# Batches 6 and 7 of the first round: their second product by seven products for eight twice, half of the weights parked in DRAM, and new orders for all engines

## The chip, the cores and the metric

One Trainium2 chip, of which the kernel uses one core: TensorE (PE; its weight loads are shown as PEld), VectorE (DVE), ScalarE (ACT), GpSimd (POOL), and SyncE (SP), which issues most DMAs. The metric is the device time of one execution in microseconds; the median of several runs counts.

## What is computed

Cross attention between tokens and states, then a feed-forward block on its result:

```python
scores = scale * x @ state^T;  a = softmax(scores);   xread = a @ state      # 512 tokens read 32 states
scores2 = scale * state @ x^T; a2 = softmax(scores2); sread = a2 @ x         # 32 states read 512 tokens
X = concatenate([xread, sread]) as (B*S, H*D)        # B = 8, S = 512 + 32, H*D = 512
h = X @ w_in                                         # 512 -> 2048
g = h * erf(softplus(h))
out = g @ w_out                                      # 2048 -> 512
```

All is float32, 8 batches, 8 heads of width 64. The output is (4352, 512).

## The kernel before

Work goes by batches of 512 tokens; the states' 256 rows come as one more piece. The 2048 inner columns are done in two rounds: round one (`u` = 0) takes the first 1024 of them for batches 1 to 7, then for the states; round two (`u` = 1) the other 1024, again for all. Batch 0 is done ahead, in one go, by straight products (L623, L630), while the weights arrive.

For batches 1 to 7 the products are fast ones: a product of 2 x 2 blocks is done by seven block products for eight, from sums of blocks which VectorE makes. In a round, a batch passes through

- the attention (`attend`, `read`, `turn_read`; in round one only), with loads of x on SP (`xq`, 64 KB pieces, and `x`),
- `mixed` (L1125), states times w_in, which stands in for the read of the states,
- `first_product` (L1224), seven block products for eight, into the `ring` (its "h" planes),
- `serf`: softplus, erf and a multiplication (L1246, L1261, L1275), and the sums `sums_a` (L1264),
- the second product, with w_out. The blocks of w_out and the differences of them that this needs are the seven weights `("W", u, 1..7)`; three of them live in tiles called `raw` (`T[1]`, `T[2]`, `T[4]`), the rest in `w_out` itself (L428 makes the differences).

The second product exists in two forms. `second_product` (L1308) does seven block products of 4 x 2 matmuls with 256 columns, 56 in all per batch, adds results in `oo` and stores two halves of the rows from SP (L1328). `twice_product` (L1464) does each of the seven by seven for eight again: 49 products of two matmuls with 128 columns, 98 in all. For this it needs sums of the left factor (four per group, L1446, into scratch views: `yt`, and `wide`, which is `xT`), and 28 differences of the inner weights (`sums_b`, L1373), kept in the half of `w_out` and `raw` that this round does not use. Its results are copied out (L1474), added (L1479, L1513), and seven quarter stores go from POOL as DMAs that accumulate in DRAM (L1508). Before the change round one uses the first form for all its batches and round two the second for all. The last batch of round two joins its results on VectorE and stores from SP.

Between the rounds come the states: `sums_states` and `first_states` (L1627), `second_states` (L1676), `put_states`, with `bring_in` (L1769), which loads the second half of w_in from DRAM (`kept_in`) into `xq` and `x`. Every batch's attention weights and their sums are parked in DRAM in round one (`keep_y`) and brought again in round two (`bring_y`).

The order of work is written out: every operation is entered by `op` with an engine, a cost, what it reads and what it writes; a table `ORDER` gives for each engine the sequence in which its operations stand, and `emit` issues them so. The orders of TensorE, VectorE and ScalarE are kept as written; DMAs wait in line on their queue. Waits come from the tiles' overlaps, not from that table. The page's lines are those of this kernel.

Of the kernel before, what the change touches and what calls it, by code (L numbers as in the profile page):

```python
# [17 lines left out]
def kernel(  # L18
# [47 lines left out]

    ring = const.tile([P, 2, 3, GF, GF, P], F32, name="ring")
# [299 lines left out]
    def mixed_pair(b, gs, first_h=False, split=False, then=lambda: None):  # L367

        for g in gs:
            m_t[b, g] = mix.tile([P, 2, gw], F32, name="m")  # L370
# [70 lines left out]
    def begins(b):  # L441
        return 1 - b % 2
# [143 lines left out]
    def groups0():  # L586
# [12 lines left out]
        def mixed_part(g, first, n, hs=range(H)):  # L599
            if (0, g) not in m_t:  # L600
                m_t[0, g] = mix.tile([P, 2, gw], F32, name="m")
# [84 lines left out]
    def next0():  # L686
# [26 lines left out]
        def mixed(j):  # L713
            g = 2 * begins(1) + j
            if not n_ps:
                for k in range(2):
                    m_t[1, 2 * begins(1) + k] = mix.tile([P, 2, gw], F32, name="m")
# [77 lines left out]
    def op(engine, cost, at, go, reads=(), writes=(), table=None, land=0.0):  # L795
# [9 lines left out]
        for r in writes:  # L805
# [6 lines left out]
            8 2 0 11 10 9 12 3 1 13-15 22 18 17 19 6 16 20 23 7 21 24-26 35-36 31 4-5 27 32-34 60  # L812
            37-39 28 40 47 59 41-43 61-62 48 44-45 49 46 63 66 29 64 51 65 68-69 52-53 70 54 67 71
            50 72 30 73 55-56 74 76 57-58 106 78-79 107 80-81 108 75 109 82-83 110 84-85 113 112 111
            90-91 116 86 77 114 87 117 88 115 92 94 118 89 93 119-120 95 98-99 96 123 121 100-101
            153 125 97 154 126 156 102-104 155 122 157 127-129 158 105 130 159-160 131 133 163 134
            132 164 137-138 162 141 161 139 124 165 140 166 135 167 136 145-146 168 170 142-143
            147-148 200 144 172-173 202 201 203 174 149-150 175 169 207 176 204 177 180 205 151-152
            210 206 181 209 171 211 182 208 184 212 183 213-214 185 178 186 179 187-188 215 217
            189-190 192-193 247 194 191 195 248 219 250 220 216 249 196 251 221 197 222 252 254 253  # L820
            198 227 257 199 256 231 258 255 223 228 260 218 259 232-233 262 229 224 261 230 225 293
            234-235 226 239 236 240 295 241-242 237 294 265 238 266 296 267 263 268 297 269 243 273
            244 270 245 298 300 299 274 302-303 271 264 246 275 304 277 335 301 276 336 306 305 272
            281 337 278-280 339 341 282 340 285 283 338 307 286 342 284 287-288 343 308 344 289 363
            309 345 290-291 310 364 292 346 315 347 316 319 317 348 323 369 320 318 370 321-322 365
            311 367 366 327 371 312 372 313 328 314 368 329 373-377 349 378 324 330 393 325 350 326
            395-396 394 400 353 397 331-332 354 398 333-334 355 403 399 351 359 404 401-402 360 406
            352 405 361 357 408 407 356 358 383 362 437 379-382 387 385 388 384 440 386 389 391 441
            439 438 390 442 444 416 392 409 447 443 446 448 418 445 417 420 410 421 419 450 412 411
            422 449 452 413 430 451 414-415 482 431 481 432 423 433 484 424 483 425 434 426 485 427  # L830
            435 486 488 436 429 428 491 460 487 461 453 492 463 489 462 490 464 454-455 494 456-457
            493 465 496 459 458 466-467 495 469 474 525 471 526 468 476 470 527-528 475 477 529 478
# [3 lines left out]
            583 553 545 554 613 562 546-547 584 563 555 564-565 557 556 558 614 559 616 566 560 617  # L836
            615 561 567 618 620 568 619 585 623 622 586 592 587 624 594 589 596 621 625 590 626-627
            593 588 595 628 597 591 598 657 606 599 658 608 607 601 609 600 659 602 610 660 603 612
            661 611 604-605 663 662 636 629 664 638 630-631 667 632-633 668 637 634 665-666 639 669
            635 640 670 641-643 650 645 644 646-647 651-654 649 655 648 671 656 673 672 674 678 675  # L840
            680 676-677 679 682 685 681 687 686 688 684 689 683 692 691 690 694 693 699 696 695 701
            697 700 703 702 698 704-705""",
        ACT: """
            4 6 5 9 7 1 0 10 8 11 13 12 30-31 15 22-23 16 14 35 17 34 3 36 32 37 33 19 21 18 20 26
            24 41 40 27 38-39 49 28 25 29 2 42-43 53 47 55 54 44 50 56 51 46 45 57 62 59 58 64 63 61
            65 52 67 66 60 69 48 68 70 76 75 71 79 77-78 72 80 73 90 74 91 86 92-93 84 94 99 81-82
            101 83 102 96 105 103 100 85 104 106 97 88 112 95 107 113 98 87 108 116 114-115 117 109
            89 127 110 129 118 128 130 111 120 123 119 121 131 136 138 133 137 139-140 132 141 122
            125 144 135 142 149 143 150 134 145 154 151-153 124 146 164 147 126 165 148 160 166 157
            155 167-168 173 158 156 175-177 174 169 171 186 178 161 187 159 162 172 170 188 190  # L850
            179-180 189 181 191 182-184 201 163 203 185 202 204 195 194 197 205 193 210 192 212-213
            206 196 211 208 214-215 218 223 225 198 224 207 199 226 217 232 209 216 219-220 200
            221-222 234 228 233 235-236 241 227 243 242 244 239 245 248 237 249 229 258 247 238 246
            240 230 250 260 251-252 231 259 261 253-254 262 264 271 266 263 256 265 273 267 274 268
            255 272 269 275 270 277 284 278 287 285 276 279 286 257 289 280-281 290 282-283 291-293
            298 300-301 299 297 294-295 302 312-313 311 306 314 305 304 296 303 307-309 335 288 337
            310 338 336 339 344 315 320 346-347 321 323 341 322 352 316 345 343 350 348 324 340
            317-318 359-360 342 357-358 330 319 349 351 353 381 354 325 355 331 383 382 356 333 326
            332 327 384 328 385 390 334 366 392 329 393 367 361 389 362 388 386 369 368 391 364 363
            370 394 406 387 405 398 397 365 371 395 403-404 372 396 376 427 399-400 374 401-402 373  # L860
# [5 lines left out]
            529 525 536 541 501 507 524 506 527 544 503 508 542-543 534 514 535 509 526 533 565 537  # L866
            515-516 538-539 510 517 567 540 512 566 568 511 518 569 550 513 545 551 574 571 546 576
            548 572 570 549 577 547 575 579 552 573 578 553 581 580 582 554-555 583 556 584 560
            585-586 557 561 558 562-563 559 587 564 588 592 590 589 593 595 591 597 594 598 600 599
            596 602 601 603 607 605 608 604 606 610 609 611""",  # L870
        DVE: """
            0-1 38 16 15 14 17 2-3 39-40 24-26 6-7 4 19 18 21 36-37 20 22-23 5 27-30 32 34 31 33 35
            10 74 52 46 11 51 8 53 50 13 9 42 12 61 43 48 60 75 62 47 77 41 54 56 76 44 58 49 55 57
            59 81 73 63-65 67 45 66 82 69 71 68 72 70 101 83 121 123 78 99 84 100 102 122 79 85 93
# [38 lines left out]
    def emit():  # L913
# [21 lines left out]
        order = sorted(begin, key=lambda n: (begin[n], n))  # L935
        for n in order:
            ops[n][3]()

    made_banks = {}

    def bank(name):
# [916 lines left out]
```

## Time and profile before

| What | Value |
|---|---|
| Time, median of 3 runs | 709.88 us (709.11 to 709.97) |
| The profiled execution: time | 709.91 us |
| its span, first to last instruction | 708.1 us |
| Granted TensorE clock | 1.000 |
| Last matmul's end | 703.5 us |
| Second product of round one, first matmul per batch 1 to 7 | 129.5, 175.5, 218.2, 259.9, 302.9, 342.9, 385.7 us |
| L1308, PE rows (two for each matmul of the source) | 784 of 128x256 |
| L1464, PE rows | 1372 of 128x128 |
| SP's queue | 33.9% of 16 DMA engines' time, 64.25 MB |
| POOL's queue | 12.9%, 11.01 MB, all after 485 us |

The first 100 us are batch 0 and the loading of weights; 100 to about 440 us is round one, with the states' pieces towards its end; from about 470 us round two. A matmul's busy time contains its pipeline, and rows overlap: what one costs is the distance from its start to that of the next.

### The profile page before, as it was taken

What the parts mean: (1) busy time and instruction counts of PE and PEld (TensorE: products, weight loads), DVE (VectorE), ACT (ScalarE), POOL (GpSimd) and SP (SyncE); (2) the same over time, 40 slices, a digit from 0 to 9 for tenths busy, and PEclk for the clock granted to TensorE, in tenths of its full rate; (3) what the DMA queues carried; (4) which work ended last, traced back from release to release, by engine and by line L of the source; (5) the groups of instructions that cost most, each with busy time, mean ns of one, the idle gap of its engine ahead of it and who ended that gap; (6) DMA issues with size and microseconds to landing.
All of it is one profiled execution on the core that took longest, in us unless ns stands there. A gap on an engine that the chain in (4) does not pass through costs nothing.

```text
span 708.1 us, 12453 instructions
## 1 busy us (share of the span) xinstructions
PE 699.9 (99%) x4871; PEld 563.7 (80%) x4871; DVE 539.3 (76%) x852; ACT 465.4 (66%) x782; POOL 51.6 (7%) x48
## 2 busy tenths in 40 slices
PE   8999999999999999999999999999999999999997
PEld 7444346687878788787899988888989898989997
DVE  6997887988969688485735426499768776978897
ACT  4999898958587665757263463738485756666742
POOL 0000000000000000000000000001113222212222
PEclk9999999999999999999999999999999999999999
DMA  8869582756835464353320001104246535526555
GB/s 259 254 193 248 198 187 54 148 94 144 224 90 111 95 170 122 95 174 78 113 82 31 31 23 60 52 31 80 33 82 67 106 34 96 74 33 78 86 89 106
DMA packets 156011, 76.58 MB, mean 108 GB/s; under 512 B 123440, under 2 KB 145456, under 8 KB 155440
## 3 DMA queue, kind: packets, MB, share of 16 engines
q1 hardware_dynamic: 143984, 64.25, 33.9%
q0 software_dynamic: 11424, 11.01, 12.9%
q8 instruction: 38, 0.62, 0.4%
q10 hardware_dynamic: 544, 0.52, 0.2%
q14 instruction: 21, 0.17, 0.1%
HBM read 42.60 MB, written 29.49 MB: 102 GB/s over the span
## 4 chain that ended last, share of the span: by engine, by line
PE 93%; DMA 3%; SPq 1%; ACT 1%; DVE 1%; issue 1%; ACTq 0%; DVEq 0%
PE o L1308 24%; PE o L1464 21%; PE h L1224 16%; PE o L630 7%; PE at L1224 6%; PE o L1676 3%; PE h L1627 3%; PE at L623 2%; PE h L623 2%; PE at L1125 2%; PE h L1125 2%; DMA raw<-in_moe_w_out_dram 2%; SPq L360 1%; PE at L1627 1%; PE at L1087 1%; PE h L984 1%
## 5 line engine op out<-in xcount | busy, mean ns | idle before, releaser
L1236 ACT COPY ring<-h 128x512 f32<-128x512 f32 x112 | 64.8, 587 | 100.5 <-PE h L1224 95.4
L1308 PE MATMUL o<-w_out,ring 128*128 128x256 f32 x448 | 110.3, 381 | 0.0
L1264 DVE TENSOR_TENSOR ring<-ring 128x1024 f32<-128x1024 f32 (+1 forms) x60 | 68.2, 1145 | 42.3 <-ACT ring L1261 42.3
L1308 PEld LDWEIGHTS o<-w_out,ring 128*128 128x128 f32 x448 | 83.4, 190 | 17.5 <-issue 5.9
L1224 PE MATMUL h<-aT,m 128*128 128x256 f32 x336 | 85.9, 380 | 0.0
L1308 PE MATMUL o<-raw,ring 128*128 128x256 f32 x336 | 82.8, 381 | 0.0
L1308 PEld LDWEIGHTS o<-raw,ring 128*128 128x128 f32 x336 | 62.7, 190 | 12.9 <-issue 5.0
L1246 ACT ACTIVATE ring<-ring 128x512 f32<-128x512 f32 x112 | 66.9, 630 | 6.0 <-DVE ring L1242 1.8
L1224 PEld LDWEIGHTS h<-aT,m 128*128 128x128 f32 x336 | 61.6, 190 | 8.2 <-ACT ring L1236 0.3
L1275 DVE TENSOR_TENSOR ring<-ring 128x1024 f32<-128x1024 f32 x56 | 67.8, 1217 | 0.3
L1464 PE MATMUL o<-w_out,w_in 128*128 128x128 f32 x448 | 60.6, 276 | 0.0
L1464 PEld LDWEIGHTS o<-w_out,w_in 128*128 128x128 f32 x448 | 56.5, 192 | 4.4 <-issue 1.7
L630 PE MATMUL o<-w_out,ring 128*128 128x512 f32 x128 | 59.3, 599 | 0.0
L1261 ACT ACTIVATE ring<-ring 128x1024 f32<-128x1024 f32 (+1 forms) x60 | 58.6, 1002 | 0.2
L630 PEld LDWEIGHTS o<-w_out,ring 128*128 128x128 f32 x128 | 23.6, 190 | 28.9 <-issue 27.4
L1464 PE MATMUL o<-w_out,ring 128*128 128x128 f32 x336 | 46.0, 276 | 0.0
L1508 POOL DMA_DIRECT2D out_dram<-ot x6 | 7.9, 1309 | 516.6 <-DVE w_out L1373 484.2
L1464 PEld LDWEIGHTS o<-w_out,ring 128*128 128x128 f32 x336 | 42.5, 192 | 3.2 <-ACT ot L1474 0.8
L1464 PE MATMUL o<-raw,ring 128*128 128x128 f32 x252 | 34.9, 276 | 0.0
L1464 PEld LDWEIGHTS o<-raw,ring 128*128 128x128 f32 x252 | 32.3, 192 | 1.5 <-DVE w_in L1446 0.8
L1238 DVE TENSOR_TENSOR ring<-ring,at 128x512 f32<-128x512 f32 x28 | 19.1, 683 | 17.5 <-ACT ring L1236 6.4
L1464 PE MATMUL o<-raw,xT 128*128 128x128 f32 x224 | 29.3, 276 | 0.0
(268 smaller groups left out, 1301.6 us busy)
## 6 DMA issues: line engine op xcount, KB each, us to landing
raw<-in_moe_w_in_dram SPq DMA_DIRECT2D x16, 512.0 KB, 4.9
raw<-in_moe_w_out_dram SPq DMA_DIRECT2D x8, 1024.0 KB, 5.7
xq<-in_x_dram SPq DMA_DIRECT2D x112, 64.0 KB, 2.6
x<-in_x_dram SPq DMA_DIRECT2D x56, 128.0 KB, 3.4
out_dram<-oo SPq DMA_DIRECT2D x14, 512.0 KB, 3.2
kept_a<-aT SPq DMA_DIRECT2D x7, 512.0 KB, 3.3
aT<-kept_a SPq DMA_DIRECT2D x7, 512.0 KB, 3.3
out_dram<-oo POOLq DMA_DIRECT2D x12, 256.0 KB, 4.6
```

The lines of the kernel that those rows point to most:

```text
L623: nc.tensor.matmul(out=h_t[g, i], lhsT=m_t[0, g][:, e, P * i:P * i + P], rhs=aT[0][:, e], start=start, stop=not start)
L630: nc.tensor.matmul(out=acc[r], lhsT=gT[g][:, i, P * r:P * r + P], rhs=w_out[:, GF * g + i, :], start=(made_of[r] == 1), stop=(made_of[r] = ...
L1125: nc.tensor.matmul(out=bank(names[e])[q, :], lhsT=st[r, b, q], rhs=of_group[2 * u + j][r, :, i, :], start=True, stop=True)
L1224: nc.tensor.matmul(out=out_[:, i], lhsT=x_[:, q:q + P], rhs=y_, start=(start and i == 0), stop=(i == 1), skip_group_check=not start)
L1236: op(ACT, 0.5, t, lambda: nc.scalar.copy(out_(), view(bank(name))), [name], w)
L1246: op(ACT, 0.53, t, lambda: nc.scalar.activation(out=part(splane, k), in_=part(hplane, k), func=ACTF.Softplus), area(hplane, ks=[k], os=[o] ...
L1261: op(ACT, 0.085 + 0.875 * share, at + n, lambda s_=s_: nc.scalar.activation(out=s_, in_=s_, func=ACTF.Erf), [], area(splane, ks=[k], os=os ...
L1264: op(DVE, 0.065 + 1.075 * share, at + n + 1, lambda s_=s_, h_=h_: tt(s_, s_, h_, op=ALU.mult), area(hplane, ks=[k], os=os), area(splane, k ...
L1275: op(DVE, 1.14, at + k, lambda k=k, x_=x_, y_=y_, how=how: tt(get("h", k), get(*x_), get(*y_), op=how), area(v[x_[0]], ks=[x_[1]]) + area( ...
L1308: nc.tensor.matmul(out=view(name)[:, h], lhsT=lhs[:, i, :], rhs=weight_of[n]()[:, u, i, :], start=(start and h == 0 and i == 0), stop=(h = ...
L1464: nc.tensor.matmul(out=out_[:, Q2 * k:Q2 * k + Q2], lhsT=lhs[:, k, i], rhs=rhs[:, i], start=first, stop=(k == len(ns) - 1 and i == 1), ski ...
L1627: nc.tensor.matmul(out=bank(bk)[:, P * i:P * i + P], lhsT=x_[:, i, k], rhs=y_[:, k], start=(start and i == 0 and k == 0), stop=(i == GF - ...
```

## The change

Of batches 6 and 7 in round one the second product is done by `twice_product`. This needs a place for the 28 inner differences, which is the half of `w_out` and `raw` that holds round two's weights. So these weights are made earlier, written to DRAM (`keep_w`, four DMAs on SP, placed when batch 2 is at its second product), and brought back after batch 7 (`bring_w`), before the states' second half. Other scratch: `xq`, the `m` tiles and `xT` for the sums of factors; `oo`, `ot`, `x`, `sc` and an `m` tile for results. The four `m` buffers become one tile `mm_t`, so that neighbouring ones can be used as one; `sums_states` and `first_states` of the first half stand some 11 us earlier and use `aT0` and `oo` in the place of an `m` tile and `xT`. In round one the first store to each quarter of a batch's rows is a plain one from SP, the other three accumulate from POOL. The orders of all five engines are new throughout; the operations entered for other batches are the same.

```diff
+    mm_t = mix.tile([P, 4, 2, GF * P], F32, name="m", bufs=1)
...
-    mt = lambda j: kept_tile("m%d" % j, lambda: mix.tile([P, 2, gw], F32, name="m"))
+    mt = lambda j: mm_t[:, j]
...
-    def sums_b(at):
+    def sums_b(u, at):
         def chunk(n):
-            t = w_out[:, 0:NF // 2].rearrange("p i e -> p (i e)").rearrange(
-                "p (n x) -> p n x", n=4)[:, n - 1] if n < 5 else \
-                T[(1, 2, 4)[n - 5]][:, 0].rearrange("p i e -> p (i e)")
+            t = w_out[:, NF // 2 * (1 - u):NF // 2 * (2 - u)].rearrange(
+                "p i e -> p (i e)").rearrange("p (n x) -> p n x", n=4)[:, n - 1] if n < 5 else \
+                T[(1, 2, 4)[n - 5]][:, 1 - u].rearrange("p i e -> p (i e)")
...
+    kept_w = dram.tile([P, (NF // 2) * d_model + 3 * GF * E2], F32, name="kept_w")
+
+    def weights_of(u):
+        first = NF // 2 * d_model
+        parts = [(w_out[:, NF // 2 * u:NF // 2 * (u + 1)].rearrange("p i e -> p (i e)"),
+                  kept_w[:, 0:first])]
+        for k, n in enumerate((1, 2, 4)):
+            q = first + GF * E2 * k
+            parts.append((T[n][:, u].rearrange("p i e -> p (i e)"), kept_w[:, q:q + GF * E2]))
+        return parts
+
+    W_of = lambda u: [("W", u, n) for n in range(1, 8)]
+    B_of = lambda u: [("B", u, n, m) for n in range(1, 8) for m in range(4, 8)]
+
+    def keep_w(at):
+        op(SP, 2.4, at, lambda: [nc.sync.dma_start(out=k, in_=t) for t, k in weights_of(1)],
+           W_of(1), ["kept_w"], land=16.0)
+
+    def bring_w(at):
+        op(SP, 2.4, at, lambda: [nc.sync.dma_start(out=t, in_=k) for t, k in weights_of(1)],
+           ["kept_w"], W_of(1) + B_of(0), land=16.0)
+
-    def twice_product(b, splane, hplane, inner, at, at_s, final=None):
+    def twice_product(b, u, splane, hplane, inner, at, at_s, final=None):
...
+        else:
+            first = lambda: static["xq"].rearrange("p i m d -> p (i m d)").rearrange(
+                "p (x m i t) -> p x m i t", x=2, m=4, i=2) if par == 0 else \
+                mm_t[:, 0:2].rearrange("p x e (m i t) -> p x (e m) i t", m=2, i=2)
+            yt = lambda x0, x1: first() if x0 == 0 else mt(3).rearrange(
+                "p e f -> p (e f)").rearrange("p (x m i t) -> p x m i t", x=1, m=4, i=2)
...
+            elif not u and not par:
+                t = static["x"].rearrange("p (z c) h d -> p z (c h d)", z=2)[:, g - 2].rearrange(
+                    "p (x e) -> p x e", x=2)
...
-        def put(v, r, c, t):
+        def put(v, r, c, t, plain=False):
+            if plain and not u:
+                op(SP, 0.5, t, lambda: nc.sync.dma_start(out=quad(r, c), in_=one(v)),
+                   every(*v), [("out", b, r, c)], land=3.5)
+                return
...
-        put(R1, 0, 0, at + 8)
-        put(R4, 1, 0, at + 11)
+        put(R1, 0, 0, at + 8, True)
+        put(R4, 1, 0, at + 11, True)
...
-        put(R3, 0, 1, t)
+        put(R3, 0, 1, t, True)
         put(R7, 1, 0, t)
-        put(R5, 1, 1, t)
+        put(R5, 1, 1, t, True)
...
-        if u == 0:
+        if u == 0 and b < TWICE:
             second_product(b, u, splane, hplane, base, at_s)
         else:
-            twice_product(b, splane, hplane, inner, base, at_s,
-                          3 - hplane if b == B - 1 else None)
+            twice_product(b, u, splane, hplane, inner[u], base, at_s,
+                          3 - hplane if u and b == B - 1 else None)
+        after(base)
...
+    TWICE = B - 2
...
             if b == 2:
                 sums_w(1, base + 20, 1, 2, 4, 3)
+                keep_w(base + 30)
...
-                first_states(0, 0, nxt - U + 14, names[0])
+                first_states(0, 0, nxt - U + 3, names[0])
+        if b == TWICE:
+            adopt(W_of(1), B_of(0))
+            inner[0] = sums_b(0, base - 10)
...
     second_states(0, 0, base)
+    bring_w(base)
```

`adopt(names, into)` enters no operation any more; it makes later users of one set of names wait for those of the other.

More of the change, by code (lines that the diff above doesn't have):

```diff
@@ L817 @@
[L817 to L827, printed above, removed]
@@ L937, in emit, with adopt @@
             ops[n][3]()
+    def adopt(names, into):
+        every = [*names, *into]
+        used = sorted({n for r in every for n in [*wrote.get(r, ()), *seen.get(r, ())]})
+        for r in every:
+            wrote[r], seen[r] = used, []
     made_banks = {}
@@ L1438, in place @@
                 if m in (5, 6, 7, 3):
-                    return [("Y", slot, m)]
+                    return [("Y", 0, 4, m)] if not u and par and not slot else [("Y", u, slot, m)]
                 h, ih = {1: (0, 0), 2: (0, 1), 8: (1, 0), 9: (1, 1)}[m]
@@ L1469, in mm @@
                 op(PE, 0.447 * len(ns), t, go,
-                   place(9 if m == 4 else m) + [("W", 1, n) if m < 4 else ("B", n, m) for n in ns],
+                   place(9 if m == 4 else m) + [("W", u, n) if m < 4 else ("B", u, n, m) for n in ns],
                    [of_bank[to]])
@@ L1729, with unit @@
     sums_w(0, BASE, 1, 2, 4, 3)
-    def unit(b, u, base, splane, hplane, follow, between):
+    def unit(b, u, base, splane, hplane, follow, between, after=lambda base: None):
         at_s = base + 14
@@ L1743 @@
     hp = {b: 2 if b % 2 else 0 for b in range(1, B)}
+    TWICE = B - 2
+    sums = (3, 5, 6, 7)
+    parts = lambda par, g: [("R", par, g, x_, h, q) for x_ in range(2) for h in range(2)
+                            for q in range(2)]
+    inner, names = {}, {}
     for b in range(1, B):
@@ L1770, in bring_in @@
                                           in_=kept_in[:, GF * j:GF * j + GF])
-                op(SP, 0.2, base + 4, bring_in, [],
-                   ["x", "xq"] + ["xq%d" % i for i in range(NI)] + ["w_in10", "w_in11"], land=8.0)
-                names[0] = sums_states(0, base + 4)
-                sums_reads(base + 8)
-        names = {}
+                    op(SP, 0.5, base + 4, bring_in, [], [k, "w_in1%d" % j] + used, land=7.0)
+                adopt([("Y", 0, 1, m) for m in sums], [("mS", 1, 0), ("mS", 1, 1)])
+                adopt(parts(0, 0), ["oo00", "oo01"])
+                names[0] = sums_states(0, base - 8)
+                sums_reads(base - 6)
         def follow(nxt, b=b):
@@ L1782, in follow @@
             else:
-                first_states(0, 0, nxt - U + 14, names[0])
-        unit(b, 0, base, 1, hp[b], follow, between)
+                first_states(0, 0, nxt - U + 3, names[0])
+        if b == TWICE:
+            adopt(W_of(1), B_of(0))
+            inner[0] = sums_b(0, base - 10)
+            adopt(["xq"] + ["xq%d" % i for i in range(NI)], [("Y", 0, 0, m) for m in sums])
+            adopt(["xT%d" % k for k in range(4)], [("Y", 0, 2, m) for m in sums])
+            for par in range(2):
+                adopt(["oo%d%d" % (r, c) for r in range(2) for c in range(2)], parts(par, 0))
+            adopt([("mS", 0, e) for e in range(2)], parts(1, 2))
+        if b == B - 1:
+            adopt(["m%d%d" % (j, e) for j in range(2) for e in range(2)],
+                  [("Y", 0, 4, m) for m in sums])
+        unit(b, 0, base, 1, hp[b], follow, between, after)
     base = BASE + U * (B - 1)
     second_states(0, 0, base)
+    bring_w(base)
+    adopt([("Y", 0, 4, m) for m in sums], ["m%d%d" % (j, e) for j in range(2) for e in range(2)])
+    adopt([("Y", 0, 2, m) for m in sums], ["xT%d" % k for k in range(4)])
+    adopt(parts(1, 2), [("mS", 0, 0), ("mS", 0, 1)])
+    adopt(parts(1, 0), ["oo10", "oo11"])
     bring_y(1, base - 20)
```

236 lines of the change are left out of this document (128 added, 108 removed), and 11 rows, old and new, of the table ORDER.

## The prediction

> **What bounds the kernel now.** I read the page's engine shares and slices first, then the chain of work that ended last, then the list of who waited for whom, cut to TensorE from 100 us on.
>
> ```profile
> PE 699.9 (99%) x4871; PEld 563.7 (80%) x4871; DVE 539.3 (76%) x852; ACT 465.4 (66%) x782; POOL 51.6 (7%) x48
> ...
> PE   8999999999999999999999999999999999999997
> ...
> DVE  6997887988969688485735426499768776978897
> ACT  4999898958587665757263463738485756666742
> ...
> PE 93%; DMA 3%; SPq 1%; ACT 1%; DVE 1%; issue 1%; ACTq 0%; DVEq 0%
> PE o L1308 24%; PE o L1464 21%; PE h L1224 16%; PE o L630 7%; PE at L1224 6%; PE o L1676 3%; PE h L1627 3%; PE at L623 2%; PE h L623 2%; PE at L1125 2%; PE h L1125 2%; DMA raw<-in_moe_w_out_dram 2%; SPq L360 1%; PE at L1627 1%; PE at L1087 1%; PE h L984 1%
> ...
> PE at L1100 <- ACT sT L1103: 0.5, 1, 0.5
> ```
>
> TensorE is busy in every slice but the first and last, 93% of the chain is its work, and in the 600 us after 100 us it waits once, 0.5 us, for another engine. So time here is the sum of TensorE's spacings; VectorE (DVE) and ScalarE (ACT) have room that is uneven, least in the first half of round one and most in slices 20 to 26.
>
> Busy time of one matmul (381 or 276 ns) counts its pipeline; what it costs is start to start. From TensorE's timeline, unbroken stretches of the two second products:
>
> ```profile
> 326.16 2.75 PE L1308 MATMUL o<-raw,ring 128*128 128x256 f32 x12
> 328.75 1.03 PE L1308 MATMUL o<-w_out,ring 128*128 128x256 f32 x4
> ...
> 681.16 2.84 PE L1464 MATMUL o<-w_out,w_in 128*128 128x128 f32 x24
> 683.84 1.06 PE L1464 MATMUL o<-w_out,ring 128*128 128x128 f32 x8
> ```
>
> Twelve matmuls of 256 columns take 2.59 us (0.216 each), twenty-four of 128 columns 2.68 us (0.112 each). Each matmul of the source is two such rows (784 rows at L1308 for 7 batches of 56).
>
> **The change, part by part.** *Removed from TensorE:* for batches 6 and 7, 112 rows each by 0.216 = 24.2 us. *Added:* 98 matmuls, 196 rows, by 0.112 = 22.0 us. The gain is 2.2 to 2.3 us a batch; with the unrounded spacings (2.59/12, 2.68/24) 24.17 - 21.89 = 2.3, for two batches 4.6 us. Bounds: the chain's longest unbroken piece of L1464, 32.02 us for 283 rows, gives 0.1131 and 22.2 us, so 4.0 us together; the two lines' shares of the chain as its ordered view has them (24.3% and 21.4% of 708.1 over 7 batches each: 24.6 and 21.6) give 5.9 us. I take 4.6, the spacing itself, since the shares also hold what stood between.
>
> [...]
>
> *Added to VectorE, ScalarE, POOL and SP, off the path:* the spacing of a 128x256 op is 0.333 us, of 128x512 0.60, from this stretch of its timeline:
>
> ```profile
> 453.54 0.42 DVE L1373 TENSOR_TENSOR raw<-w_out 128x256 f32<-128x256 f32 x1
> 453.87 0.76 DVE L1373 TENSOR_TENSOR w_out<-w_out 128x256 f32<-128x256 f32 x2
> 454.54 0.68 DVE L1136 TENSOR_TENSOR sx<-sx,m 128x512 f32<-128x512 f32 x1
> 455.14 0.68 DVE L1136 TENSOR_TENSOR m<-m 128x512 f32<-128x512 f32 x1
> ```
>
> The 28 differences of the inner weights: 28 x 0.333 = 9.3. Per batch, 12 wide and 4 narrow sums of factors 12 x 0.60 + 4 x 0.333 = 8.5; 6 adds of 0.333 and 2 of about 0.20 (narrower still) = 2.4; four totals of 0.60 = 2.4; less three adds of 0.60 = 1.8. Together 9.3 + 2 x 11.5 = 32.3 us. It must fit between some 263 and 460 us. ACT gets 40 short copies (8 of them bank to bank) for 8 long ones, a few us. What room there is, by stage:
>
> ```profile
> 126.00:263.00 137.00, 136.52 (x992) 107.97 (x991) 116.73 (x196) 96.64 (x162) 0.00 (x0) 1.00 0.61 136
> 263.00:340.00 77.00, 77.00 (x470) 62.91 (x469) 56.59 (x89) 49.46 (x80) 0.00 (x0) 1.00 0.42 114
> 340.00:460.00 120.00, 120.00 (x768) 105.39 (x768) 58.33 (x80) 59.01 (x93) 0.00 (x0) 1.00 0.16 54
> 460.00:700.00 240.00, 240.00 (x1863) 220.66 (x1862) 198.90 (x327) 149.30 (x305) 50.94 (x42) 1.00 0.46 69
> ```
>
> Columns after the length are busy us of PE, PEld, DVE, ACT, POOL, then clock and DMA share. From 263 to 460 DVE is idle 20.4 + 61.7 = 82 us, so 32.3 lies beside TensorE. In round two (last row) DVE is busy 83% with the same kind of product and TensorE still has no gap; that is the cover at work. Were it gone entirely, the cost would be the 32.3 us.
>
> *Moved:* the four weight differences of round two (L428, 1.22 us each, now at 278, 316, 330 and 358 us) come before batch 4's read, since they must be parked before their place is taken. That puts 4.9 us into the stage 126 to 263, where DVE has 20.3 us idle; I cost it at nothing, and the second rival at what it is if that room can't be used. *Parking:* four DMAs on SP, 2048 + 3 x 512 KB, issued behind batch 4's sixteen small DMAs (201 to 212 us) and ahead of batch 6's `xq` load, on one queue whose landings come in the order of issue. The nearest rows are the writes of w_in to DRAM, 1 MB each:
>
> ```profile
> kept_in<-ring SPq DMA_DIRECT2D x2, 1024.0 KB, 6.5
> ...
> xq<-kept_in SPq DMA_DIRECT2D x1, 1024.0 KB, 6.1
> x<-kept_in SPq DMA_DIRECT2D x1, 1024.0 KB, 5.8
> ```
>
> The second of them landed 2.5 us after the first (89.9 and 92.4 us). So 3.5 MB takes from 3.5 x 2.5 = 9 to, at the slower one's 8.5 us, 30 us. I take 9, back to back as here. Then `xq` lands at about 225 instead of 222.4 us, and its first transposition came at 231.4: no cost. At 30 us it lands near 245, 14 us late, and DVE, which takes its orders in line, holds everything behind the transposition.
>
> *Bringing back:* the big DMA (2 MB) waits for the last matmul of batch 7's product. Before the first matmul that needs it stand, in the changed order of TensorE, two mixing blocks (1.0 us), 14 pairs of L1224's kind and 12 of L1676's (26 x 0.864 = 22.5): 23.5 us. The 1 MB loads took 5.8 and 6.1 us; two of them end to end, 12 us, is the upper bound, so it is hidden with 11 us to spare. SP's loads of batch 1's factors are issued behind the first two of these DMAs; they have some 11 us of matmuls ahead of them and need about 6.
>
> *Stores:* per batch four plain quarter stores on SP and three accumulating ones on POOL, whose queue is empty in round one (4.6 us to landing in round two), for two half stores. Batch 6's last results lie in `x`, which then takes w_in's second half: four totals and what stands between on DVE (9 us), an accumulating store (1.2 + 4.6), the load (5.8) make 21 us after batch 6's last matmul; by TensorE's order the first reader stands 25 us behind it. The one tile for the four `m` buffers, the reused `aT0` and `oo`, and the earlier start of the first states product change what waits for what, not the work; nothing in the order puts them on TensorE's path.
>
> Sum: 709.91 (this execution; its span is 708.1, and 1.8 lies around it) - 4.6 = 705.3. The median of the runs is 709.88, so no correction is due. Start and tail (4.6 us from the last matmul's end) stay.
>
> **The rivals.** (1) *The gain goes into waits on transfers at the turn of the rounds*: if the accumulating stores take 7.4 us to landing and 2.2 to issue, as the slowest in round two did, the `x` chain's 21 becomes about 25, no room left, and what little is late on DVE passes to TensorE; 2 to 4 us come back, 707 to 709. For: DVE is in order and waits there. Against: 4 us of room at the median. If as much as the whole gain is lost it ends within 0.2%.
> (2) *Slower: VectorE can't do the moved work in time.* Summing each order's spacings from batch 1's scaled read to batch 4's last multiplication by erf (L1275), DVE does 135.5 us in the new order against 126.7, and TensorE comes to that place 1.7 us earlier. That takes 10.5 of the 18 us that DVE idles up to there (126.5 to 271.3 us). For: much of DVE's idle time is waiting for ACT (42 us before L1264 over the whole kernel), which other work fills only if it stands in the right place. Against: TensorE never waited for DVE here. If only a fifth, 3.7 us, can be used, TensorE is 6.8 us late: 712.1. It decides from below 5.9 us. The `xq` load at its slow bound would do about the same.
> (3) *Weight loads set the pace of the narrow tiles*: at the 0.19 us that one load lasts in the trace (192 ns), 196 rows cost 37.6 us, 13.4 more than now, twice: 736.7. [...]
>
> **How the numbers follow.** The forecast 705.3 has 0.69 (its own range 704.0 to 705.9, from the gains 5.9 and 4.0); rival 1 has 0.18, of which 0.08 ends within 0.2%; rival 2 0.12; rival 3 0.01. A difference under 0.2% (1.4 us) can't be told from none here. So faster 0.69 + 0.10 = 0.79, same 0.08, slower 0.13. The range is 704.0 to 709.5: it holds the forecast and rival 1, and leaves out rival 2 and what is odd.
>
> **What would show it.** Right: 1764 matmul rows in the place of L1464 at 0.112 us, 560 in the place of L1308, TensorE without waits between 130 and 700 us, DVE above 60% busy in slices 20 to 25, and the parking DMAs' landing before batch 6's transpositions. Wrong: TensorE waiting for DVE between 180 and 270 us (rival 2), for `x`, `w_out` or `raw` by DMA near 390 to 450 us (rival 1), or a spacing near 0.19 us (rival 3).

## The result and the profile after

The changed kernel takes 704.79 us (median of 4 runs, 704.68 to 705.37), the one before beside it 709.57 (4 runs, 709.11 to 709.97): a ratio of 0.9934, 95% interval 0.9917 to 0.9952, or 3.4 to 5.9 us. The prediction was 705.3. The profiled execution took 704.70 us with a span of 702.9.

Lines have moved: L1308 is now L1321, L1464 is L1508, L1224 L1237, L1373 L1383, L1125 L1138, L977 L990, L1627 L1676, L1676 L1725. From the page after, the engine shares, the slices of PE, DVE and ACT, and the chain that ended last:

```profile
PE 694.6 (99%) x5039; PEld 565.4 (80%) x5039; DVE 571.8 (81%) x930; ACT 469.3 (67%) x812; POOL 58.9 (8%) x54
...
PE   8999999999999999999999999999999999999997
...
DVE  6997887999979788696969753896979587778997
ACT  5999898949576655838473455846585756666842
...
PE 94%; DVE 4%; issue 0%; ACT 0%; DVEq 0%; ACTq 0%
PE o L1508 28%; PE o L1321 17%; PE h L1237 17%; PE o L631 8%; PE at L1237 7%; PE o L1725 3%; PE h L1676 3%; PE h L624 2%; PE at L624 2%; PE h L1138 2%; PE at L1138 2%; PE at L1676 1%; PE at L1100 1%; PE h L997 1%; PE at L613 1%; DVE ring L1568 1%
```

VectorE's busy time rose by 571.8 - 539.3 = 32.5 us (32.3 were forecast), and most of the light slices 20 to 26 are fuller. Two of them are not: from 404 to 439 us the digits are 5 and 3 (they were 2 and 6), below the 60% that the prediction named as a sign. TensorE is still the chain; a part of it has gone over from the 256-column form (L1321) to the 128-column one (L1508). The list of whom TensorE waited for, from 100 us on, has two entries:

```profile
PE at L1113 <- ACT sT L1116: 0.7, 1, 0.7
PE at L1138 <- DVE ring L1255: 0.2, 1, 0.2
```

They stand at 128.3 and 129.7 us, ahead of the first piece of moved work (169.2 us), so none of that ended up on the path. A part of the 4% of DVE in the chain lies there too: it goes back over VectorE from 131 to 116 us, where three of round one's own weight differences (L429) now stand side by side. Busy time by stage (columns: length, then PE, PEld, DVE, ACT, POOL, clock, DMA share, GB/s):

```profile
126.00:263.00 137.00, 135.99 (x989) 106.94 (x989) 122.13 (x204) 92.66 (x156) 0.00 (x0) 1.00 0.63 144
263.00:340.00 77.00, 77.00 (x535) 63.54 (x534) 62.42 (x110) 49.69 (x81) 0.00 (x0) 1.00 0.45 128
340.00:460.00 120.00, 120.00 (x895) 110.55 (x894) 86.24 (x140) 67.47 (x126) 7.38 (x6) 1.00 0.36 105
460.00:700.00 240.00, 238.24 (x1869) 219.87 (x1868) 197.38 (x326) 149.60 (x310) 50.84 (x42) 1.00 0.45 72
```

DVE's column went from 116.7, 56.6 and 58.3 to 122.1, 62.4 and 86.2 us. The last stage's is as it was.

Start to start, the rows of L1508 are 0.112 us apart (median; 1764 rows) and those of L1321 0.216 (560 rows); the mean busy time of one is 0.276 and 0.382. At these spacings the change of form is worth 2 x (112 x 0.216 - 196 x 0.112) = 4.5 us. The span fell by 5.2. Of the other 0.7 us, 0.5 lies in the first 20 us, where the kernel before had a 0.32 us wait of L623 for ACT at 20.5 us. Seven of the twelve runs below, six of them with the changed kernel's start, have waits of 0.2 to 0.7 us at that place too, so they go with the execution and not with the change.

### The profile page after: what moved, and what is told of

It reads as the page before. It is cut to its first block, busy times and chain, and to the rows that moved or that the text cites. A ratio compares the mean times of both kernels' runs of the same rounds, so it can differ in the third digit from the quotient of the medians.

```text
span 702.9 us, 12986 instructions
## 1 busy us (share of the span) xinstructions
PE 694.6 (99%) x5039; PEld 565.4 (80%) x5039; DVE 571.8 (81%) x930; ACT 469.3 (67%) x812; POOL 58.9 (8%) x54
## 4 chain that ended last, share of the span: by engine, by line
PE 94%; DVE 4%; issue 0%; ACT 0%; DVEq 0%; ACTq 0%
PE o L1508 28%; PE o L1321 17%; PE h L1237 17%; PE o L631 8%; PE at L1237 7%; PE o L1725 3%; PE h L1676 3%; PE h L624 2%; PE at L624 2%; PE h L1138 2%; PE at L1138 2%; PE at L1676 1%; PE at L1100 1%; PE h L997 1%; PE at L613 1%; DVE ring L1568 1%
## 5 line engine op out<-in xcount | busy, mean ns | idle before, releaser
L1237 PE MATMUL h<-aT,m 128*128 128x256 f32 x336 | 85.1, 380 | 0.0
L1321 PE MATMUL o<-w_out,ring 128*128 128x256 f32 x320 | 77.7, 383 | 0.0
L1321 PEld LDWEIGHTS o<-w_out,ring 128*128 128x128 f32 x320 | 59.6, 190 | 15.9 <-issue 5.9
L1237 PEld LDWEIGHTS h<-aT,m 128*128 128x128 f32 x336 | 61.8, 190 | 10.4 <-ACT ring L1249 0.8
L1508 PE MATMUL o<-w_out,w_in 128*128 128x128 f32 x448 | 59.6, 275 | 0.0
L1321 PE MATMUL o<-raw,ring 128*128 128x256 f32 x240 | 58.9, 381 | 0.1
L1508 PE MATMUL o<-w_out,ring 128*128 128x128 f32 x432 | 58.8, 276 | 0.0
L1508 PEld LDWEIGHTS o<-w_out,ring 128*128 128x128 f32 x432 | 54.1, 192 | 4.2 <-issue 1.7
L1508 PEld LDWEIGHTS o<-w_out,w_in 128*128 128x128 f32 x448 | 56.0, 192 | 1.7 <-issue 0.8
L1556 POOL DMA_DIRECT2D out_dram<-oo x14 | 17.0, 1213 | 448.5 <-ACT o L1529 360.8
L1321 PEld LDWEIGHTS o<-raw,ring 128*128 128x128 f32 x240 | 45.3, 190 | 9.5 <-issue 2.5
L631 PEld LDWEIGHTS o<-w_out,ring 128*128 128x128 f32 x128 | 23.7, 190 | 27.6 <-issue 26.2
L1508 PE MATMUL o<-raw,ring 128*128 128x128 f32 x324 | 44.7, 276 | 0.0
L1508 PEld LDWEIGHTS o<-raw,ring 128*128 128x128 f32 x324 | 41.3, 192 | 2.4 <-issue 1.7
L1251 DVE TENSOR_TENSOR ring<-ring,at 128x512 f32<-128x512 f32 x28 | 19.1, 684 | 23.5 <-ACT ring L1249 21.8
L1508 PE MATMUL o<-raw,xT 128*128 128x128 f32 x288 | 37.3, 275 | 0.0
```

The source lines that it names most:

```text
L631: nc.tensor.matmul(out=acc[r], lhsT=gT[g][:, i, P * r:P * r + P], rhs=w_out[:, GF * g + i, :], start=(made_of[r] == 1), stop=(made_of[r] = ...
L1237: nc.tensor.matmul(out=out_[:, i], lhsT=x_[:, q:q + P], rhs=y_, start=(start and i == 0), stop=(i == 1), skip_group_check=not start)
L1321: nc.tensor.matmul(out=view(name)[:, h], lhsT=lhs[:, i, :], rhs=weight_of[n]()[:, u, i, :], start=(start and h == 0 and i == 0), stop=(h = ...
L1508: nc.tensor.matmul(out=out_[:, Q2 * k:Q2 * k + Q2], lhsT=lhs[:, k, i], rhs=rhs[:, i], start=first, stop=(k == len(ns) - 1 and i == 1), ski ...
```

## The experiments

Each kernel below is the changed one with one edit, but for one that edits the kernel before. The first two were timed seven and eleven times, the others once; beside them the kernel before took 709.28 to 710.62 us.

**The old form in the new orders.** Batches 6 and 7 go back to 56 matmuls of 256 columns; parking, `sums_b(0)` and the order of the other operations stay. The old form has fewer operations, so the tables `ORDER` had to be written anew for all five engines, with its operations merged in. In the first run the states' first product also takes `xT` again in the place of `oo`. In the second run `FORM` is 7, so batch 6 alone goes back.

```diff
-        if u == 0 and b < TWICE:
+        if u == 0 and b < FORM:
...
+    FORM = 8
```

> The changed kernel with one part undone: batches 6 and 7 of round one use the 56-matmul form again (their operations put into the new orders at the places of the old ones); the 28 inner differences are still made, the weights still parked and brought back, all other orders kept. Theory A (the time is the sum of TensorE's spacings, and the gain is 448 rows of 0.216 us against 784 of... in short 2 x 112 x 0.216 against 2 x 196 x 0.112): 4.6 us slower than the changed kernel, 709.4, up to 711.5 if the merged order brings waits. Theory B (the gain comes from the orders found anew, not from the form): within 1 us of 704.8. Theory C (the form saves more, but side work such as differences and parking gives part of it back): over 711 without TensorE waits.

> As the run before, but only batch 6 is put back to the 56-matmul form; batch 7 keeps the 98-matmul form. A: half the gain is gone, 704.8 + 2.3 = 707.1, up to 709 with waits of the merged order. B: within 1 us of 704.8. If the gain of a second batch is hidden by something else (the states' chain at the turn of the rounds), 704.8 to 705.5 or 709 and more.

Both back: 712.02 us (7 runs), 1.0028 of before, interval 1.0017 to 1.0040. One back: 710.85 (11 runs), 1.0013, 1.0005 to 1.0022. Both are over what theory A allowed (711.5 and 709), the second so far that by its number alone it would fit "709 and more", the gain of the second batch hidden by something else. Their traces say why: with the old form in places made for the new one TensorE waits where the changed kernel doesn't (theory C asked for a time over 711 without such waits). The lists of whom TensorE waited for, first of the run with both back:

```profile
PE o L1316 <- DVE oo L1330: 1.8, 1, 1.8
```

and with one back:

```profile
PE o L1318 <- DVE oo L1332: 1.7, 1, 1.7
...
PE o L1505 <- DVE oo L1332: 0.8, 1, 0.8
...
PE o L1505 <- ACT o L1526: 0.3, 1, 0.3
```

In distance from start to start these cost 1.96 us in the first run (at 371.7) and 1.83 + 0.94 + 0.50 = 3.27 in the second. Spans are 709.8 and 708.8 against 702.9. Less the waits, 4.9 and 2.6 us stand against the changed kernel: two forms and one, as the prediction has them (4.6 and 2.3), within 0.3 us. And the first run less its wait, 707.8, is the span of before, 708.1: by this subtraction the new orders bring nothing by themselves, against theory B, and the form brings the gain. As measured, new orders with the old form were 2.2 us slower than the kernel before. The new form in the old orders was not tried.

**No parking.** The four DMAs to DRAM and the four back are left out, so round two works with weights that have been overwritten.

```diff
-        op(SP, 2.4, at, lambda: [nc.sync.dma_start(out=k, in_=t) for t, k in weights_of(1)],
+        op(SP, 2.4, at, lambda: None,
...
-        op(SP, 2.4, at, lambda: [nc.sync.dma_start(out=t, in_=k) for t, k in weights_of(1)],
+        op(SP, 2.4, at, lambda: None,
```

> The eight parking DMAs are left out: round two's weights are neither written to DRAM nor brought back (round two then multiplies by what the inner differences left there). A (transfers are hidden): within 0.6 us of the changed kernel, span 702.3 to 703.5. Rival (the transfers cost something, by queueing ahead of the xq load or by the wait for w_out): faster by 1 us or more.

704.78 us, span 703.0. Parking costs nothing that can be measured.

**Half of the new products.** Of the two matmuls of each of the 49 products one is left out in round one: 98 rows a batch fewer, 21.9 us for both.

```diff
-                        for i in range(2):
+                        for i in range(2 if u else 1):
...
-                                start=first, stop=(k == len(ns) - 1 and i == 1),
+                                start=first, stop=(k == len(ns) - 1 and i == (1 if u else 0)),
```

> In the 98-matmul products of batches 6 and 7 of round one the second matmul of each pair is left out (half of the inner sum is missing there): 196 rows fewer by 0.112 us, 21.9 us less work on TensorE, everything else the same. If TensorE alone bounds that stage and the others had ample room: 683. If VectorE and ScalarE are close behind (86 us of DVE work in 120 us, now in 98): TensorE begins to wait and the time is 685 to 694. If one of them is already the bound: over 697, less than a third of the 21.9 us.

696.29 us, span 694.5: 8.4 us less, between the second of the expected cases (685 to 694) and the third (over 697, VectorE or ScalarE already the bound). The other 13.5 us went between 344 and 405 us. Nine waits there make 8 us of idle time by TensorE's list, and cost 9.7 us from start to start; another 2 us are some twenty rows that stand 0.2 to 0.3 us apart instead of 0.112. What made up the rest was not worked out. The largest waits:

```profile
PE o L1508 <- DVE ot L1523: 2.4, 1, 2.4
PE o L1508 <- ACT x L1518: 2.3, 2, 1.4
PE at L1113 <- DVE sn L1106: 1.2, 1, 1.2
...
PE o L1508 <- DVE oo L1523: 0.8, 1, 0.8
```

These are the copies and sums of the results (L1518, L1523) and the softmax of the states. In this stretch only 8.4 of 21.9 us less TensorE work showed: VectorE and ACT, idle as they look, did not follow a much faster TensorE.

**More VectorE work where the weight differences were put.** Three of round two's differences are done four times each.

```diff
-            op(DVE, 1.14, at, lambda n=n: combine_w(u, n), [("W", u, k) for k in reads],
+            op(DVE, 1.14, at, lambda n=n: [combine_w(u, n) for _ in range(4 if u and n != 3 else 1)],
+               [("W", u, k) for k in reads],
```

> The changed kernel with 10.4 us more VectorE work at the place of the moved weight differences: three of round two's weight differences (169, 188 and 212 us) done four times each (9 x 1.15 us), results unchanged. Theory A (cover: VectorE's idle pieces there are real room): VectorE idles 12 us from 160 to 250 us in the changed kernel, so it is at most some 5 us late near 220 us, has caught up by 250, and TensorE waits for it under 1.5 us: 704.0 to 706.5 us. Rival B (that idle time cannot be used, a fifth at most): 10.4 less 2.4, 8 us of waits for VectorE in TensorE's list between 180 and 270 us: 711 to 715 us.

714.13 us, span 712.4, 9.5 us longer. The dose was larger than planned: repeated on the same tile, these operations stand 1.26 us apart, so nine of them are 11.3 us and not 10.4. Theory A fell. The time is in rival B's range, and the waits stand where it says, but they make 5.8 us of idle time, not 8; 1.8 us are rows at half speed, of which the last section tells. TensorE's list:

```profile
PE at L1237 <- DVE sx L1149: 2.5, 1, 2.5
PE h L1237 <- ACT h L1207: 2.1, 1, 2.1
PE h L997 <- DVE xq L990: 1.2, 1, 1.2
```

The two traces laid beside each other, operation by operation: when VectorE is 3.8 us late, at the transposition of 170.3 us, TensorE is 1.8 late at the matmul that reads it; when VectorE is 10.2 late, after 212 us, TensorE is 9.1 late. So VectorE is 2.0 and 1.1 us ahead of need at these places, though it idles 12 us from 160 to 250.

**More VectorE work in the inner differences.** Each of the 28 of round one is done four times, and twice in a later run.

```diff
-                op(DVE, 0.335, at + n / 2, lambda n=n, o=o, x_=x_, y_=y_: tt(
-                    inner(n, o), inner(n, x_), inner(n, y_), op=ALU.subtract),
+                op(DVE, 0.335, at + n / 2, lambda n=n, o=o, x_=x_, y_=y_: [tt(
+                    inner(n, o), inner(n, x_), inner(n, y_), op=ALU.subtract)
+                    for _ in range(1 if u else 4)],
```

> The changed kernel with each of the 28 inner weight differences of round one done four times: 84 x 0.333 = 28 us more VectorE work between 234 and 364 us, results unchanged. VectorE idles 32 us from 230 to 400 us there. Theory A: most of it fits, TensorE waits 0 to 6 us: 704 to 711 us. Rival B (a fifth of the idle time can be used): 28 less 6, 22 us late: 723 to 728 us. Between the two, the time says which share of the idle pieces is room.

> The changed kernel with each of the 28 inner weight differences of round one done twice: 9.3 us more VectorE work between 234 and 364 us (with 28 us more it was 21.3 us longer). Theory F (a threshold: a few us of room, passed on one for one above it): 28 less 21.3 is 6.7 us of room, so 0 to 4 us is passed on: 704.7 to 709 us. Rival H (a fixed share, 0.76 of whatever is added): 7.1 us: 711 to 713 us. Rival A (32 idle us are room): under 0.6 us.

Here too the doses were larger than planned. VectorE's timeline, first in the changed kernel and then with four of each:

```profile
234.43 0.40 DVE L1383 TENSOR_TENSOR raw<-w_out 128x256 f32<-128x256 f32 x1
234.76 0.68 DVE L1048 TENSOR_TENSOR xT<-xT,z 128x512 f32<-128x512 f32 x1
...
234.78 1.78 DVE L1383 TENSOR_TENSOR raw<-w_out 128x256 f32<-128x256 f32 x4
236.48 0.68 DVE L1048 TENSOR_TENSOR xT<-xT,z 128x512 f32<-128x512 f32 x1
```

One holds VectorE for 0.33 us, four for 1.70: each repetition on the same tile costs 0.46. Over all 28 the doses are 38.6 us (not 28) and 12.9 (not 9.3).

Four times: 726.05 us, span 724.3, 21.4 us longer, so 17 of the 38.6 were taken up, or 20 if the 3 us of rows at half speed are left out. The time is in rival B's range only because the dose was larger: of the 32 us that VectorE idles here, more than half could be used, not a fifth. Twice: 707.96, span 706.2, 3.3 us longer, so 9.6 of 12.9 were taken up. This is in theory F's range, but its threshold does not fit both runs (17 us of room would have taken up all 12.9), and a fixed share, rival H, does not either (0.55 of 12.9 is 7.1 us). With twice the work the largest part is one wait, the matmul that needs the states' softmax at 354 us:

```profile
PE at L1113 <- DVE sn L1106: 1.8, 1, 1.8
```

**The same dose in both kernels.** Eight reductions of 1.1 us, 8.8 us in one block, ahead of the same transposition in the changed kernel and in the one before.

```diff
-                op(DVE, 0.62, scored_at - 6, lambda i=i: nc.vector.transpose(
-                    out=xT()[:, i], in_=xT()[:, i]), ["xq"], ["xq%d" % i])
+                op(DVE, 0.62, scored_at - 6, lambda i=i: [nc.vector.reduce_max(
+                    out=spare, in_=st[:, 1:B].rearrange("p b n -> p (b n)"), axis=AX.X)
+                    for _ in range(8 if b == 4 and i == 2 else 0)] + [nc.vector.transpose(
+                    out=xT()[:, i], in_=xT()[:, i])], ["xq"], ["xq%d" % i])
```

> The changed kernel with eight extra VectorE reductions (128x896 into one spare column, results unchanged, some 7 to 9 us together) ahead of one transposition of batch 4's xq, which stands at 170.3 us. There VectorE idles 5.5 us from 170 to 210. The run with more weight differences showed TensorE waiting as soon as VectorE was 1.1 to 1.5 us late. Theory F (the change used up the room of this stage, about 1.5 us is left): TensorE ends 5.5 us late or more: 710 to 714 us. Rival A (the idle pieces are room): 704 to 706.5 us.

> The kernel before with the same eight reductions ahead of the same transposition, at 169.0 us there; VectorE idles 9.0 us from 169 to 210 in it. Theory F (there was room here before, and the change took it): at least 2.5 us less is passed on than in the changed kernel: 0 to 4 us over its 709.9, 709.9 to 714. Rival G (this place was as tight before, and the moved work found its room by the new order alone): the same 5.5 us or more as in the changed kernel: 715.4 to 719 us.

Changed kernel: 714.75 us, span 712.9, 10.0 longer. Before: 720.95, span 719.2, 11.1 longer. Theory F's second half fell: the kernel before passed on no less. The times are over the ranges of F and of rival G, since the block cost more than its own length. First TensorE's timeline in the changed kernel with the block (start, length, what; in brackets the idle time before and who ended it), then the wait in the one before:

```profile
173.77 1.05 PE L1000 MATMUL h<-xq,st 64*32 64x512 f32 x4
178.78 1.99 PE L1000 MATMUL h<-xq,st 64*32 64x512 f32 x4 [3.96 <-DVE xq L993]
181.10 1.93 PE L1000 MATMUL h<-xq,st 64*32 64x512 f32 x8 [0.33 <-DVE xq L993]
182.96 4.28 PE L1324 MATMUL o<-w_out,ring 128*128 128x256 f32 x13
```

```profile
PE at L1227 <- DVE ring L1241: 8.6, 1, 8.6
```

The block does not stand where it was expected (170.3 and 169.0 us), and the two orders differ around it. VectorE's timeline in the kernel before, then in the changed one, both without the block, which goes ahead of the transposition:

```profile
165.10 0.67 DVE L977 STREAM_TRANSPOSE xq<-xq 128x512 f32<-128x512 f32 x1
165.69 0.65 DVE L1238 TENSOR_TENSOR ring<-ring,at 128x512 f32<-128x512 f32 x1
...
165.14 0.69 DVE L1251 TENSOR_TENSOR ring<-ring,at 128x512 f32<-128x512 f32 x1
...
168.60 0.70 DVE L990 STREAM_TRANSPOSE xq<-xq 128x512 f32<-128x512 f32 x1
```

In the order before, an operation on `ring` that TensorE waits for stands right behind the transposition; in the new order it stands ahead of it. So the block met different consumers. In the changed kernel TensorE was 6.9 us late at the last matmul that waited, with VectorE 8.8 late: 2.0 us ahead of need, as above. In the one before, the operation on `ring` ended at 166.34 us and its matmul began at 166.95, while with the block the matmul began 0.05 us behind it: VectorE was 0.6 us ahead of need. So the old order had a tight place too, and the stage got 5.4 us more VectorE work all the same; that it was the same place, as rival G says, is not shown. The rest of the cost is rows at half speed: the four of the second line take longer than sixteen do without the wait (1.09 us).

**Parking more.** The 2 MB piece is written to DRAM once more, ahead of the four.

```diff
+    again_w = dram.tile([P, 2, (NF // 2) * d_model], F32, name="again_w")
...
-        op(SP, 2.4, at, lambda: [nc.sync.dma_start(out=k, in_=t) for t, k in weights_of(1)],
+        op(SP, 2.4, at, lambda: [nc.sync.dma_start(out=again_w[:, 0], in_=weights_of(1)[0][0])] + [
+            nc.sync.dma_start(out=k, in_=t) for t, k in weights_of(1)],
```

> The changed kernel with the 2 MB piece of the weights written to DRAM once more, ahead of the four parking transfers. Batch 6's xq, which landed at 232.2 us just before its first transposition at 232.35, then lands 6.6 to 8.8 us later, near 239 to 241. Theory A (as the prediction's step on parking says: a late xq holds VectorE and everything behind it): VectorE stands 6 to 9 us at that transposition, of which its 8 us of idle up to 271 us absorb some, and TensorE waits 1 to 6 us: 706 to 711 us. Rival C (TensorE's own order has more than 8 us in hand there): under 0.6 us of new waits, 704 to 705.5 us.

708.10 us, span 706.3: 3.4 longer, in theory A's range. VectorE's timeline at batch 6's first transposition, the changed kernel and then this one:

```profile
231.22 1.21 DVE L1288 TENSOR_TENSOR ring<-ring 128x1024 f32<-128x1024 f32 x1
232.35 0.70 DVE L990 STREAM_TRANSPOSE xq<-xq 128x512 f32<-128x512 f32 x1
```

```profile
231.50 1.22 DVE L1288 TENSOR_TENSOR ring<-ring 128x1024 f32<-128x1024 f32 x1
236.04 0.71 DVE L990 STREAM_TRANSPOSE xq<-xq 128x512 f32<-128x512 f32 x1 [3.32 <-DMA xq<-in_x_dram]
```

It began 0.08 us after the twelfth of the sixteen `xq` transfers had landed (235.96). In the changed kernel the twelfth landed at 230.13, 2.2 us ahead of need. VectorE was 3.7 us late, TensorE soon 3.5. The last transfer landed 5.9 us later than in the changed kernel (238.11 against 232.20), a little less than expected, and VectorE stood 3.3 us rather than 6 to 9, since the first transposition does not need the last four.

**Bringing back more.** The 2 MB piece is loaded three times, one after the other.

```diff
-        op(SP, 2.4, at, lambda: [nc.sync.dma_start(out=t, in_=k) for t, k in weights_of(1)],
+        op(SP, 2.4, at, lambda: [nc.sync.dma_start(out=t, in_=k)
+                                 for t, k in weights_of(1)[:1] * 2 + weights_of(1)],
```

> The changed kernel with the 2 MB piece of the weights loaded back three times, one load after the other. The one load took 8.6 us and landed at 431.0 us; the first reader stands near 441 us, some 10 us later (the prediction said 11 us to spare). Two more loads take 13 to 17 us, so the last lands at 444 to 448. Theory A (hidden with 10 to 11 us to spare): TensorE or VectorE waits 3 to 7 us for w_out: 707.5 to 712 us. Rival D (more room than that, VectorE's differences wait but TensorE does not): 704 to 706 us. Rival E (no room, the load already paces the turn): 13 us or more, over 717 us.

706.93 us, span 705.1, 2.2 longer: between A's range and D's. The wait that A named is there, shorter than it said:

```profile
PE o L1726 <- DMA w_out<-kept_w: 1.3, 1, 1.3
```

The last load landed at 447.74 us; the first reader, which stands at 445.89 in the changed kernel, began at 447.78. With the one load's landing at 430.98 the room is 14.9 us.

**The x load three times**, likewise one after the other.

```diff
-                        nc.sync.dma_start(out=flat.rearrange("p (j k) -> p j k", j=GF),
-                                          in_=kept_in[:, GF * j:GF * j + GF])
+                        for _ in range(1 if j else 3):
+                            nc.sync.dma_start(out=flat.rearrange("p (j k) -> p j k", j=GF),
+                                              in_=kept_in[:, GF * j:GF * j + GF])
```

> The changed kernel with the 1 MB load of w_in's second half into x done three times, one after the other, at the turn of the rounds. The one load landed at 391.7 us, and the first operation on x stood at 400.5 us. Two more loads take some 10 us, so the last lands near 402. Theory A (9 us of room in the x chain): TensorE waits 0 to 2 us: 704 to 706.7 us. The prediction's rival 1 (no room in this chain): 8 us or more: over 712 us.

710.23 us, span 708.4, 5.5 longer: between the two. TensorE's timeline:

```profile
399.73 1.06 PE L1508 MATMUL o<-raw,ring 128*128 128x128 f32 x8
404.36 2.82 PE L1676 MATMUL h<-sT,x 128*128 128x128 f32 x16 [3.57 <-DMA x<-kept_in]
406.97 1.06 PE L1508 MATMUL o<-raw,m 128*128 128x128 f32 x4
```

The last load landed at 404.31 (12.7 us after the first's 391.65, not 10), and the reader followed 0.05 us later; its place in the changed kernel is 400.52. So the room is 8.9 us, and all of it is room: 3.8 us of the 5.5 are this wait, 1.7 rows at half speed behind it.

## Why the prediction came out right, step by step

- **The sum of TensorE's spacings** (4.6 us): right. 4.5 at the measured spacings, 4.9 for two forms and 2.6 for one in the runs that undo them, less their waits. The 32 us of L1464 rows at 0.113 were the right row; rival 3 (0.19 us a row) has nothing for it: a weight load of L1508 lasts 0.192 us in the trace after, and the rows stand 0.112 apart all the same.
- **32.3 us of VectorE work beside TensorE**: right in size (32.5) and in outcome, but the argument was not good enough, and that it came out was partly luck. It counted 82 us of idle time as room. The runs show that how much of it is room depends on the place: in blocks, 9.5 us were passed on of 11.3 and 10.0 of 8.8; spread over 28 places, 21.4 of 38.6 and 3.3 of 12.9. That the work of the change fitted in without a wait is best put down to the order made for it, with each piece where TensorE's next need of VectorE was not yet due; no run tests this, since none puts the same work into the old order.
- **Rival 2** (VectorE can't do the moved work; it needs 10.5 of 18 us, and decides below 5.9): it did not happen, but it stood closer than 0.12 and "TensorE never waited for DVE here" make it look. That row shows a lead over zero, not its size: 0.6 us before, and 2.0 and 1.1 after, at the places tried, which are different ones.
- **Where the inner differences go** ("between some 263 and 460 us"): the first six stand at 234 to 253 us, and the last of round one at 363.7. So the stage 126 to 263 got 4.9 us of moved weight differences, as forecast, and 2.0 of these; its VectorE work rose by 5.4, so 1.5 us of other work left it.
- **Parking** (3.5 MB in 9 us, `xq` landed at about 225 us): the last of the four DMAs landed 10.9 us after the first was issued; the bound of 30 was far off. All 387 transfers of SP's queue landed in the order of their issue in the trace after, as all 375 did before. But `xq` had landed only at 232.2 (224.8 in the run without parking). That error, 7 us where the margin was 6, would have been a stall had the first transposition needed all of it. Two things were left out: SP spent 1.2 to 1.6 us on each of the first five `xq` issues behind the parking (0.49 as a rule), and `xq` is consumed in pieces. What remained was 2.2 us.
- **Bringing back** (11 us to spare): 14.9. The cover was 23.5 us as worked out (422.4 to 445.9); the load took 8.6 us where 12 was taken as a bound.
- **The x chain, and rival 1** (21 against 25 us): 8.9 us of room rather than 4. Batch 6's last accumulating store from `x` was issued at 381.5 us and landed 4.8 us later, at 386.23, near the median, and the load took 5.1. The last to land was another, a plain store from `x` on SP (382.28 to 386.44), which the chain left out; the load was issued 0.14 us behind it.

## What to carry to other kernels

When one engine is the sum, price a trade of its work by start-to-start spacing in unbroken stretches; that term was good to some tenths of a microsecond here (4.6 us forecast, 4.5 measured). For the engine that has to cover the rest, idle time in a window said only in part what could be added (some 17 us of work into 32 us of it): ask how far it runs ahead of its next consumer, which a small extra dose of work at one place and a comparison of the two traces, operation by operation, shows at once. Read the dose from the trace too: an operation repeated on its own tile took longer here than the one that it repeats (0.46 us against 0.33). A transfer's room is measured the same way, by doing it again until somebody waits.

## What the hardware showed beside this

After some of TensorE's waits its rows went at half speed for a while. In the run with more weight differences, behind the 2.1 us wait at 199.4, seven intervals took 0.427 us where 0.216 is usual, and the clock granted from 190 to 215 us was 0.93: it was 0.50 for 3.41 us from 199.79 on. TensorE's timeline:

```profile
199.41 1.75 PE L1237 MATMUL h<-sy,sx 128*128 128x256 f32 x4 [2.11 <-ACT h L1207]
200.95 3.87 PE L1322 MATMUL o<-raw,ring 128*128 128x256 f32 x12
204.66 1.03 PE L1237 MATMUL at<-sy,sx 128*128 128x256 f32 x4
```

Four such rows of L1237 take 1.03 us at full speed, as in the last line. The half speed followed every wait of 3.6 us or more seen here (3.6, 4.0, 6.0, 8.6), two of the four between 2.1 and 2.5 us (2.1 and 2.5, not 2.4 and another of 2.5), and none of 2.0 or less. Each time the granted clock was 0.50 for 3.41 us, or for 6.83 (after 4.0 and 8.6), and it cost another 1.4 to 2.5 us; so such a wait cost more here than its length. Why 2.1 us of idling was enough in one place and 2.4 in another was not, no run shows.
